# Head of the mixture-of-experts stage: row loads ahead of the last stores, gating inside the first tile's products, rows ahead of kept rows

## The chip, the cores and the metric

One core of a Trainium2 chip runs the whole program. The metric is device time in microseconds of one launch. Smaller is better. TensorE (PE) multiplies, with its weight loads beside it (PEld); VectorE (DVE) and ScalarE (ACT) do elementwise work and read the products out of PSUM; GpSimd (POOL) issues the indirect DMAs (scatters) and does some elementwise work; SyncE (SP) issues all other DMAs, in order.

## The reference

Three stages work one after the other on 8 batches of 3072 tokens of 256 numbers.

```python
X = np.fft.rfft(x, axis=1)                      # spectral mixing
Yr = Xr @ w_r - Xi @ w_i + b_r; Yi = Xr @ w_i + Xi @ w_r + b_i
Y = softthreshold(Yr, 0.01) + 1j * softthreshold(Yi, 0.01)
x = np.fft.irfft(Y, n=3072, axis=1).reshape(24576, 256)

c = x @ w_skip > 0                              # mixture of experts, 8 experts, one a token
e = argmax(x @ w_gate); g = softmax(x @ w_gate)[e]
x[c] += g * (relu(x @ w1[e]) @ w2[e])           # w1: 256x1024, w2: 1024x256

h = maximum(maximum(x @ w1, x @ w2), x @ w3)    # dense stage, 256 -> 768 -> 256
out = h @ w_out
```

## The kernel before

**Spectral stage** (`spectral`). A batch is transformed by small matrix products; the last step of a batch is a loop over `g` in 0..8. In round `g` the inverse transform `if1` (L353) makes a slice, and `to_rows` (L362) turns the slice of the round before into three blocks of 128 tokens, `yk[:, 3(g-1)]` to `yk[:, 3(g-1)+2]`, with gate scores beside the 256 numbers. Each block is stored at once to `xt` in DRAM by a 128 KB DMA (L372) on SP, so 24 stores a batch. `gating` (L379) is a generator: three steps on DVE (ten instructions, L385 to L412, which end with the mask `gm`), a step with a product for the column sums (L419) and two ACT instructions, then a step with the products L427 and L429 that give the places (nine DVE instructions, L431 to L446), after which the blocks stand in a list. `scatter(n, behind)` (L463) lets POOL wait for the tile `behind` and then scatters up to `n` blocks of the list into `rows`, a DRAM table sorted by expert.

In the last batch the gating is cut into five pieces (`LAST`, L567): blocks 0-2, 3-8, 9-14, 15-20 and 21-23. A piece is started in the round in which its last block is ready and finished in the next round.

**Experts stage** (`Experts`). It works on tiles of 256 rows of one expert. `tile` (L884) loads the tile's kept rows `xr` (`load_kept`, one DMA of 264 KB, for the residual, the gate weight and the target), then the transposed-to-be rows `xs` of the *next* tile (`load_rows`, four DMAs of 64 KB), both on SP. Four groups of 12 products each (L898, banks B, C, D, B) make `h`; after each, ACT writes `hh` (L903) and DVE `hl` (L904). After the fourth, `transposes` (L847) turns the next tile's `xs` to `xt` on DVE, splits it into `xh` (ACT) and `xl` (DVE), and `targets` makes `idx`. Then two times 24 products (L922) make `y`, and DVE makes `ob` from `y` and `xr` (L928). `tile` is a generator that yields after each group and in the middle and at the end of each half of `y`, so that its caller can put other work between. `send` (L862) scatters `ob` on POOL.

Each operand is split into a high and a low part (`h` and `l` at the end of the names); three products of them stand for one in full precision.

The first `HEAD` = 4 tiles of expert 0 (`head`, L939) are run from `spectral`'s own pools before a hardware loop over the other tiles. Their rows come from earlier batches, so their loads do not wait for the last batches' scatters. `open` (L779) loads, before the last rounds `g`, the rows of the first head tile and expert 0's weights. `get_ready(g)` (L854) splits `w1` in rounds 0 and 1, `w2` in rounds 2 and 3, and runs `transposes` for the first tile in round 4. `head` takes the last gating piece from its fourth step on, and then `table` (L969), which computes from the counts where each tile of the loop starts: DVE work on few partitions, loads of the first loop expert's weights in its second step, a product L1057 near its end. One step of that is taken at each yield of the tiles.

After the head, `loop` (L1064) runs the other tiles, and `tail` (L1092) the last two; the dense stage (`feed_forward`) follows.

What sets the order: all of this is in a manually ordered region, so each engine runs its instructions in the order of the program, and SP issues its DMAs in that order.

## Time and profile before

| | us |
|---|---|
| median of 3 runs | 2897.82 (2896.19 to 2897.95) |
| the profiled execution | 2884.95 |
| its span, first to last instruction | 2883.2 |

The profile gives times in us from the start of the span. Shares of the page: PE is busy 98% of the span, DVE 64%, ACT 48%, POOL 42%. The page's 40 slices show PE at nine tenths or more in all but three slices. The work that the change touches lies between about 744 and 857 us; the loop over the other tiles follows to about 1361, the two last tiles to 1390, and the dense stage to the end.

### The profile page before, as it was taken

How to read it: one execution, taken by the hardware profiler on the slowest of the kernel's cores; microseconds unless marked ns; L12 is line 12 of the kernel's file. 1: busy time of each engine (PE TensorE's matmuls, PEld its weight loads, DVE VectorE, ACT ScalarE, POOL GpSimd, SP SyncE). 2: the span in 40 equal slices, each digit the busy share in tenths (PEclk: the TensorE clock that was granted, in tenths of full speed). 3: DMA queues.
4: the chain of work that ended last, by engine and by line, in shares of the span. 5: the costliest groups of instructions: out<-in, count | busy, mean ns of one | idle time of the engine just before them, and what ended most of it. 6: DMA issues, size and time to landing. Idle time of an engine off the chain costs nothing.

```text
span 2883.2 us, 52001 instructions
## 1 busy us (share of the span) xinstructions
PE 2820.4 (98%) x17046; PEld 2446.7 (85%) x17047; DVE 1847.6 (64%) x2734; ACT 1381.2 (48%) x2665; POOL 1221.9 (42%) x1166
## 2 busy tenths in 40 slices
PE   9999999999979999999899999999999999999998
PEld 7888988998879999999777777777777777777776
DVE  6888788877755555555566666665666666666664
ACT  4544544454523333333455555555555555555553
POOL 2042224222542222222455555555555655555653
PEclk9999999999989999999999999999999999999999
DMA  5333333333254333333666667656677666676654
GB/s 159 102 103 114 115 116 101 107 100 101 87 179 126 103 104 97 106 96 103 136 168 159 174 171 177 169 159 170 166 179 175 164 168 160 177 173 176 160 153 106
DMA packets 401316, 400.75 MB, mean 139 GB/s; under 512 B 272634, under 2 KB 319303, under 8 KB 401140
## 3 DMA queue, kind: packets, MB, share of 16 engines
q1 hardware_dynamic: 386612, 371.63, 47.9%
q0 software_dynamic: 14528, 26.85, 2.7%
q8 instruction: 101, 1.65, 0.2%
q14 instruction: 75, 0.61, 0.1%
HBM read 309.52 MB, written 101.91 MB: 143 GB/s over the span
## 4 chain that ended last, share of the span: by engine, by line
PE 46%; DVE 3%; ACT 1%; issue 1%; DMA 1%; POOL 0%; POOLq 0%; DVEq 0%; ACTq 0%
PE pa L1216 19%; PE o_ps L1294 12%; PE pb L1216 10%; PE pc L1216 5%; DVE m L1262 1%; ACT hh L1273 1%; DVE xl L1175 1%; DMA wu<-wsc 1%; DVE m L1226 0%; ACT xh L1172 0%; DVE xc L1154 0%; DVE xt L1159 0%; POOL hl L1274 0%; DMA xt<-ob,idx 0%; POOL xt L870 0%
## 5 line engine op out<-in xcount | busy, mean ns | idle before, releaser
L1216 PE MATMUL pa<-xh,wu 128*128 128x512 f32 x1728 | 611.4, 394 | 3.4 <-ACT s L1223 2.5
L1223 ACT ACTIVATE s<-pa 128x512 f32<-128x512 f32 x648 | 378.9, 596 | 332.3 <-PE pa L1216 207.2
L1274 POOL TENSOR_TENSOR hl<-m,hh 128x512 fp32r<-128x512 f32 x288 | 400.7, 1413 | 297.1 <-ACT hh L1273 297.1
L1216 PEld LDWEIGHTS pa<-xh,wu 128*128 128x128 f32 x1728 | 324.5, 188 | 81.5 <-ACT s L1223 3.4
L1216 PE MATMUL pb<-xh,wu 128*128 128x512 f32 x864 | 345.2, 400 | 8.0 <-DVE m L1226 6.5
L1294 PE MATMUL o_ps<-hh,wo 128*128 128x512 f32 x1152 | 339.8, 397 | 3.4 <-ACT hh L1273 3.4
L1216 PE MATMUL pa<-xl,wu 128*128 128x512 f32 x864 | 339.7, 393 | 0.0
L1253 POOL TENSOR_TENSOR t<-s,s 128x512 f32<-128x512 f32 x144 | 188.3, 1308 | 258.7 <-ACT s L1223 258.7
L1294 PEld LDWEIGHTS o_ps<-hh,wo 128*128 128x128 f32 x1152 | 217.5, 189 | 54.7 <-ACT hh L1273 4.5
L1223 ACT ACTIVATE s<-pb 128x512 f32<-128x512 f32 x216 | 129.3, 598 | 265.4 <-PE pb L1216 264.9
L1262 DVE TENSOR_TENSOR m<-m,t 128x1536 f32<-128x1536 f32 x144 | 251.9, 1749 | 0.0
L903 ACT ACTIVATE hh<-h_ps 128x512 fp32r<-128x512 f32 x192 | 114.0, 598 | 267.8 <-PE h_ps L898 197.7
L904 DVE SCALAR_TENSOR_TENSOR hl<-h_ps,hh 128x512 fp32r<-128x512 f32 x192 | 131.3, 691 | 156.4 <-ACT hh L903 154.4
L472 POOL DMA_INDIRECT rows<-yk,pos x192 | 195.1, 1016 | 84.8 <-issue 59.4
L898 PE MATMUL h_ps<-xh,w1h 128*128 128x256 f32 x768 | 213.0, 277 | 7.6 <-ACT xh L145 5.1
L1216 PEld LDWEIGHTS pb<-xh,wu 128*128 128x128 f32 x864 | 162.2, 188 | 63.6 <-DVE m L1226 15.9
L922 PE MATMUL y_ps<-w2l,hh 128*128 128x256 f32 x768 | 212.9, 277 | 0.7
L898 PE MATMUL h_ps<-xl,w1h 128*128 128x256 f32 x768 | 213.0, 277 | 0.3 <-DVE xl L148 0.3
L898 PE MATMUL h_ps<-xh,w1l 128*128 128x256 f32 x768 | 212.8, 277 | 0.0
L922 PE MATMUL y_ps<-w2h,hh 128*128 128x256 f32 x768 | 212.1, 276 | 0.0
L922 PE MATMUL y_ps<-w2h,hl 128*128 128x256 f32 x768 | 212.1, 276 | 0.0
L1273 ACT ACTIVATE hh<-m 128x512 fp32r<-128x512 f32 x288 | 165.6, 626 | 82.4 <-DVE m L1262 82.4
(290 smaller groups left out, 7062.8 us busy)
## 6 DMA issues: line engine op xcount, KB each, us to landing
wu<-wsc SPq DMA_DIRECT2D x216, 896.0 KB
xc<-in_x_dram SPq DMA_DIRECT2D x64, 384.0 KB
xt<-yk SPq DMA_DIRECT2D x192, 128.0 KB
xs<-xt SPq DMA_DIRECT2D x192, 128.0 KB
out_dram<-ob SPq DMA_DIRECT2D x192, 128.0 KB
xr<-rows SPq DMA_DIRECT2D x52, 264.0 KB, 2.9
xs<-rows SPq DMA_DIRECT2D x208, 64.0 KB, 2.4
w1f<-in_moe_w_dram SPq DMA_DIRECT2D x10, 1024.0 KB
```

Of the source, the lines that this page charges most:

```text
L472: a = nc.gpsimd.indirect_dma_start(out=rows[:, :], out_offset=bass.IndirectOffsetOnAxis(ap=pos, axis=0), in_=yk[:, t, G:G + RW], in_offset ...
L898: nc.tensor.matmul(p[:, j], lhsT=a[:, k, f0:f0 + 128], rhs=v[:, k], start=(i == 0), stop=(i == 5))
L903: nc.scalar.activation(out=self.hh[:, sl], in_=p, func=AF.Relu)
L904: nc.vector.scalar_tensor_tensor(out=self.hl[:, sl], in0=p, scalar=0.0, in1=self.hh[:, sl].bitcast(F32), op0=ALU.max, op1=ALU.subtract,)
L922: nc.tensor.matmul(y, lhsT=a[:, c, 128 * j:128 * j + 128], rhs=v[:, c], start=(i == 0), stop=(i == 23))
L1216: nc.tensor.matmul(o, lhsT=self.w[:, g, at:at + 128], rhs=v[h], start=(start and i == 0), stop=(i == 2), skip_group_check=True,)
L1223: nc.scalar.activation(out=self.s[k], in_=o, func=AF.Copy)
L1253: nc.gpsimd.tensor_tensor(out=self.t[:, 2], in0=self.s[5], in1=self.s[7], op=ALU.add)
L1262: nc.vector.tensor_tensor(out=m[:, 0:3], in0=m[:, 0:3], in1=self.t, op=ALU.max)
L1273: nc.scalar.activation(out=hh[:, i], in_=m[:, i], func=AF.Copy)
L1274: nc.gpsimd.tensor_tensor(out=hl[:, i], in0=m[:, i], in1=hh[:, i].bitcast(F32), op=ALU.subtract)
L1294: nc.tensor.matmul(o, lhsT=wo[g][:, 2 * p + c, 128 * k:128 * k + 128], rhs=h[v][:, (0, 3, 1, 2)[2 * t + c]], start=(p == 0 and i == 0), st ...
```

## The change

- `load_kept` of the first head tile moves to `open`, behind its `load_rows` and ahead of the weights.
- `get_ready`: `transposes` of the first tile moves from round 4 to round 0, and behind it stands `load_rows` of the second head tile, ahead of the batch's 24 stores on SP. The splits of `w1` move to rounds 1 and 2, of `w2` to rounds 3 and 4.
- Round 8 no longer advances any gating. The fourth and later steps of the piece 15-20 and all of the piece 21-23 go into `head`, one step at a yield of the first tile; `table` follows.
- `tile` loads the next tile's rows ahead of the kept rows, in the loop and the tail too, and yields once behind the loads. The first head tile loads nothing.
- The scatters of a head tile, two and two, go behind the first and the fourth group of products (before: the first and the third).
- The loads of the first loop expert's weights move from `table`'s second step to the start of the third head tile, behind its row loads. `table` takes one more yield, so that L1057 goes to the middle of the second tile's first half of `y`.

```diff
-            queue = []
+            queue, gates = [], []
@@ rounds g of the last batch
-                        if late:
+                        if late and g < 8:
                             next(late[1], None)
                         if g in LAST:
-                            for _ in late[1] if late else ():
+                            for _ in late[1] if late and g < 8 else ():
                                 pass
                             late = [g, gating(b, *LAST[g])]
-                            for _ in range(3):
+                            gates.append(late[1])
+                            for _ in range(3 if g < 8 else 0):
                                 next(late[1])
-                        elif late:
+                        elif late and g < 8:
...
-            ex.head(bank, late[1], scatter)
+            ex.head(bank, gates[-2:], scatter)
@@ open
         self.load_rows(self.head_rows[0], True)
+        self.load_kept(self.head_rows[0], True)
         self.load_w1(0)
@@ get_ready
-        if g < 2:
-            self.split_w1(512 * g, 512 * g + 512)
-        elif g < 4:
-            self.split_w2(4 * g - 8, 4 * g - 4, True)
-        elif g == 4:
+        if g == 0:
             self.transposes()
+            self.load_rows(self.head_rows[1], True)
+        elif g < 3:
+            self.split_w1(512 * g - 512, 512 * g)
+        elif g < 5:
+            self.split_w2(4 * g - 12, 4 * g - 8, True)
@@ tile
-        self.load_kept(kept(), early[0])
         if ahead:
             self.load_rows(ahead(), early[1])
+        if kept:
+            self.load_kept(kept(), early[0])
+        yield None
...
-        if ahead:
+        if turn:
             self.transposes()
@@ head
         def rest():
-            yield from gate
-            yield
-            yield from ends
+            for n, g in enumerate(gates):
+                if n:
+                    for _ in range(3):
+                        next(g)
+                yield
+                next(g)
+                yield
+                for _ in g:
+                    pass
+                yield
+            yield from self.table(bank)
...
             for n, behind in enumerate(now):
-                if behind is not None and n % 2 == 0:
+                if n == 0:
+                    if j == HEAD - 2:
+                        for _ in rest:
+                            pass
+                        self.first_weights()
+                    continue
+                if behind is not None and n in (1, 4):
                     scatter(2, behind)
                 next(rest, None)
@@ table
-        e_first = self.value(first_i, E - 1, [ET.SP])
-        self.load_w1(e_first)
-        self.load_w2(e_first)
+        self.first_i = first_i
...
         yield
+        yield
         p = bank("A", (3, NTMAX))
         nc.tensor.matmul(p, lhsT=ones, rhs=q)
@@ new
+    def first_weights(self):
+        e_first = self.value(self.first_i, E - 1, [ET.SP])
+        self.load_w1(e_first)
+        self.load_w2(e_first)
```

## Rows read from the trace of the kernel before

**Rows 1.** Windows: us, then busy us (x instructions) of PE, PEld, DVE, ACT, POOL; clock, DMA.
```profile
806.70:857.10 50.40, 37.59 (x291) 36.00 (x291) 25.24 (x73) 11.81 (x20) 17.41 (x26) 0.83 0.61 191
857.10:1360.70 503.60, 502.90 (x4416) 501.29 (x4416) 263.17 (x459) 170.46 (x290) 133.74 (x200) 1.00 0.38 107
```

**Rows 2.** Timeline of PE: start, us, line, [idle before <- releaser].
```profile
785.76 0.24 PE L419 MATMUL bankA<-ones,gm 128*54 128x128 f32 x1 [1.46 <-DVE gm L412]
...
791.66 0.24 PE L419 MATMUL bankA<-ones,gm 128*54 128x128 f32 x1 [1.05 <-DVE gm L412]
...
792.48 0.39 PE L898 MATMUL bankB<-xh,w1h 128*128 128x256 f32 x1
...
796.12 0.22 PE L419 MATMUL bankA<-ones,gm 128*27 128x128 f32 x1 [2.00 <-DVE gm L412]
...
815.02 0.58 PE L898 MATMUL bankB<-xh,w1h 128*128 128x256 f32 x1 [8.35 <-ACT xh L145]
...
821.82 1.39 PE L1057 MATMUL bankA<-q,ones 8*128 8x318 f32 x2 [3.36 <-DVE q L1038]
```

**Rows 3.** Windows, PE alone: the third head tile.
```profile
834.18:845.06 10.88, 10.88 (x98) 1.00 0.66 212
```

**Rows 4.** Windows at the changes of the granted clock, columns as in the first group.
```profile
795.40:809.08 13.68, 10.54 (x87) 10.31 (x87) 4.45 (x18) 2.17 (x5) 4.66 (x9) 1.00 0.48 131
809.08:826.14 17.06, 7.62 (x28) 6.20 (x29) 8.09 (x42) 1.23 (x2) 4.55 (x7) 0.50 0.44 140
...
1379.10:1382.51 3.41, 3.08 (x14) 2.92 (x14) 1.29 (x4) 0.10 (x1) 1.39 (x3) 0.50 0.31 74
```

**Rows 5.** Timeline of SP, DMA issues: the last load of `open`, stores, head loads.
```profile
750.50 0.45 SPq L815 DMA_DIRECT2D w2f<-in_moe_w_dram  x1
769.15 35.56 SPq L372 DMA_DIRECT2D xt<-yk  x24
804.92 1.15 SPq L844 DMA_DIRECT2D xr<-rows  x1
806.34 3.09 SPq L839 DMA_DIRECT2D xs<-rows  x4
```

**Rows 6.** Timeline of DVE: gating of blocks 21-23, the second tile's transposes, the table, a late `hl`.
```profile
794.32 0.18 DVE L385 TENSOR_TENSOR glg<-yk 128x27 f32<-128x27 f32 x1
...
795.82 0.16 DVE L412 TENSOR_SCALAR gm<-gcmp 128x3 fp32r<-128x3 f32 x1
...
813.59 0.71 DVE L848 STREAM_TRANSPOSE xt<-xs 128x512 f32<-128x512 f32 x1 [11.21 <-DMA xs<-rows]
...
815.70 0.10 DVE L975 MEMSET sums<- 8x48 f32 x1
...
821.42 0.26 DVE L1038 TENSOR_SCALAR q<-grid,own 8x106 f32<-8x106 f32 x1
...
840.52 0.69 DVE L904 SCALAR_TENSOR_TENSOR hl<-bankB,hh 128x512 fp32r<-128x512 f32 x1 [0.67 <-ACT hh L903]
```

**Rows 7.** Timeline of SP and PE in the tail.
```profile
1371.58 0.36 SPq L844 DMA_DIRECT2D xr<-rows  x1
1372.57 2.96 SPq L839 DMA_DIRECT2D xs<-rows  x4
...
1378.87 0.40 PE L898 MATMUL h_ps<-xh,w1h 128*128 128x256 f32 x1 [5.06 <-ACT xh L145]
```

**Rows 8.** One loop tile: SP's issues, DVE's `idx` and next `hl`; last, the DMA view.
```profile
892.15 0.34 SPq L844 DMA_DIRECT2D xr<-rows  x1
893.18 3.13 SPq L839 DMA_DIRECT2D xs<-rows  x4
...
900.83 0.17 DVE L937 CAST idx<-xr 128x2 int32<-128x2 f32 x1 [0.52 <-DVEq L1086]
...
903.67 0.69 DVE L904 SCALAR_TENSOR_TENSOR hl<-h_ps,hh 128x512 fp32r<-128x512 f32 x1 [1.58 <-ACT hh L903]
...
xr<-rows SPq DMA_DIRECT2D x52, 264.0 KB, 2.9
```

More of the change, by code (lines that the diff above doesn't have):

```diff
@@ L882, in send, with tile @@
             tc.declare_no_dep(a.ins, group="sent", reason="no token is in two tiles")
-    def tile(self, hps, yps, kept, ahead=None, weights=None, next_w1=None, early=(False, False), idx_last=False):
+    def tile(self, hps, yps, kept, ahead=None, weights=None, next_w1=None, early=(False, False), idx_last=False, turn=True):
         nc = self.nc
-        self.load_kept(kept(), early[0])
         if ahead:
             self.load_rows(ahead(), early[1])
+        if kept:
+            self.load_kept(kept(), early[0])
+        yield None
         for c in range(4):
@@ L937, in targets, with head @@
         self.nc.vector.tensor_copy(out=self.idx, in_=self.xr[:, :, 257:258].rearrange("p s o -> p (s o)"))
-    def head(self, bank, gate, scatter):
+    def head(self, bank, gates, scatter):
         hps = lambda c: bank("BCDB"[c], (2, TM))
         yps = lambda j: bank("CD"[j], (D,))
-        ends = self.table(bank)
         def rest():
-            yield from gate
-            yield
-            yield from ends
+            for n, g in enumerate(gates):
[9 more added lines that the diff above has]
+            yield from self.table(bank)
         rest = rest()
@@ L957, in head @@
                 self.send()
+            ahead = None
+            if last:
+                ahead = lambda: self.value(self.t_row[0:1, 0:1], E * CAP - TM, [ET.SP])
+            elif j:
+                ahead = lambda: self.head_rows[j + 1]
             now = self.tile(
-                hps, yps, lambda: self.head_rows[j],
-                (lambda: self.value(self.t_row[0:1, 0:1], E * CAP - TM, [ET.SP])) if last
-                else (lambda: self.head_rows[j + 1]),
+                hps, yps, (lambda: self.head_rows[j]) if j else None, ahead,
                 None, self.split_w1 if last else None, (True, not last), last,
@@ L1100, in tail @@
             self.send()
-            for _ in self.tile(self.hps, self.yps, lambda: row(nt + 1)):
+            for _ in self.tile(self.hps, self.yps, lambda: row(nt + 1), turn=False):
                 next(prepare, None)
```

## The prediction

> **What bounds the kernel now.** I read the windows first. In the loop over the tiles PE is busy for 502.90 of 503.60 us, so nothing but fewer products would help there; in the 50.4 us before it, which hold the last three head tiles, PE is busy for 37.59 us, at a mean granted clock of 0.83 [rows 1]. The change works on this stretch and on the some 20 us ahead of it. Next I read PE's timeline there, for what ended each wait [rows 2]. Three times PE reaches a gating piece's column sums (L419) before DVE has made the mask `gm`: 1.46, 1.05 and 2.00 us. Then it waits 8.35 us for the second head tile's `xh`, and in that tile 3.36 us for the table's `q` ahead of L1057. An undisturbed head tile, the third, takes 10.88 us for its 96 products, 0.113 us for one [rows 3].
>
> The 8.35 us are SP's. The 24 stores of the last batch keep SP busy from 769.15 for 35.56 us, to 804.7. Behind them stand the first tile's kept rows, at 804.92, and only then the second tile's rows, at 806.34, which land at 813.59, 4.2 us after their last issue [rows 5, 6]. The table's first DVE work stands behind these transposes on DVE (815.70), and so `q` (821.42 to 821.68) comes late too: the 3.36 us have the same root [rows 2, 6]. The clock pays once more: it is granted at 0.50, the 1.2 GHz level, from 809.08 to 826.14 [rows 4].
>
> **What the change removes.** (1) *The second tile's rows* go to SP in round 0, when the first tile's transposes have freed `xs`. SP issues nothing between the last weights at 750.50 and the first store at 769.15 [rows 5], and four issues take about 3.1 us. They cost nothing as long as DVE reaches the transposes in that gap; if it doesn't, each late us delays the stores by as much. So tile 2 finds its `xh` ready: **-8.35**. (2) *The table* no longer stands behind a DMA: most of the 3.36 goes; what is left is worked out in (6). **-3.36**. (3) *The half clock* of 809.08 to 826.14. The second tile starts at 815.02 and the third at 834.18 [rows 2, 3], 19.16 us; less 10.88 and the wait of 3.36 that is 4.9, of which L1057 itself, 1.39 us at the lower clock, is worth 0.7 at the higher. **-4.2**. (4) *The first two mask waits.* In round 4 the transposes with their detour over ACT make way for a split of `w2`, and DVE can begin the piece 9-14 about 1.3 us earlier: the same transposes hold DVE for 2.1 us at 813.59 to 815.70, with ACT's `xh` in the middle [rows 6], and a split has no such detour. Of 1.46 I leave 0.2, bounds 0 and all of it. The wait of 1.05 ahead of tile 1 goes, since that product now stands behind tile 1's second group, 2.7 us later. The third wait, 2.00, moves to (5). **-1.3 -1.05 -2.00.** Together -20.2 us.
>
> **What it adds.** (5) *A longer mask wait in tile 1.* The piece 21-23 has its three DVE steps at the yield behind the fourth group, and its product L419 in the middle of `y`'s first half, 12 products or 1.36 us of PE time later. On DVE that mask stands behind the group's `hl` and behind the second tile's transposes and `idx`. From the last product of a fourth group to the end of its `hl`: tile 3 starts at 834.18, 48 products later is 839.6, and its `hl` ends at 841.21, so 1.6 us [rows 3, 6]. The nine instructions that finish the piece 15-20 stand ahead of that `hl` and overlap with its wait: +0.6, an estimate from the ten mask instructions, which take 1.66 us (794.32 to 795.98). From the transposes to the end of `idx` 2.1 us (813.59 to 815.70), of which ACT's `xh` is a part. The mask: 1.66 [rows 6]. That is 6.0 us, 6.15 with a semaphore, against 1.36: **PE waits 4.8 us**. The bounds are 3.9 (nothing of the finishing in the way, no gaps) and 5.5 (all of it in the way). Nothing hides it: PE has no other work in its order. Queued behind L419 are the rest of `y` and all later tiles.
>
> (6) *L1057* in the middle of the second tile's first `y` half: from the table's first instruction to the end of `q` DVE needs 6.0 us in the trace (815.70 to 821.68, two `ob` among them) [rows 6]; now it has from the end of tile 1's first `y` half to there, about 2.7 + 5.4 + 1.4 = 9.5 us, with four `hl`, two `ob` and the finishing of 21-23 between, about 5. A wait of **0.2**, bounds 0 and 1.5.
>
> (7) *The clock after 4.8 us without a product.* No row shows a wait of that size inside a tile. Behind the 5.06 us in the tail the clock is at 0.50 for 3.41 us; behind the 8.35 us for 17.06; behind the 2.00 us it stays at 1.00 [rows 2, 4, 7]. 4.8 is nearest to 5.06: 3.41 us at half the clock cost 3.41 x 0.5 = **1.7**. Bounds 0 and, with 17.06 us, 8.5. The Trainium skill (TensorE: Matmul & The Clock Gate, section "Why this matters for your kernels") warns of idle gaps between bursts in mid-kernel, because they bring the lower clock back; the trace agrees with the two dips above. It speaks against this change, which closes one long gap and leaves one of middle size; without the rule the time would be 1.7 lower.
>
> (8) *What is moved and costs nothing.* The early kept rows (264 KB) and row loads lie ahead of the first store. In tile 2 SP issues tile 3's rows at 804.9, where the kept rows stood; 3.1 us of issue and 4.2 to land make 812.2, and 2.1 us later, 814.3, tile 3 could start [rows 5, 6]. By the sum it starts later: tile 1 at about 789.3 (792.5 less the waits of (4) and the gating products that moved), tile 2 16.6 us later (10.88, 0.5 of gating products, 4.8, and 0.4 for smaller gaps) at 805.9, tile 3 another 11.8 later at 817.7, with the dip 819.4. So the stores hide behind the new wait, with 3 to 5 us to spare. The weights of the first loop expert now stand behind tile 4's rows; from there to their split behind tile 4's fourth group are some 14 us, and 2 MB at the 212 GB/s of [rows 3] take 10. If they came later, the loop's first tile would wait for the rest. POOL scatters the same number of blocks, the second pair one group later.
>
> (9) *The loop and the tail.* Rows ahead of kept rows change nothing for a PE that is busy throughout [rows 1]. In the tail, PE's 5.06 us end with `xh` of the last tile, whose rows SP issues at 1372.57 behind the kept rows at 1371.58 [rows 7]: they come 1.0 us earlier, **-1.0**. Bounds 0 and 1.0, since the kept rows' own issue is all that can be won.
>
> **The sum.** -20.2 + 4.8 + 0.2 + 1.7 - 1.0 = -14.5 us. The durations are those of the profiled execution (2884.95, span 2883.2), which was 12.9 under the median of the runs, 2897.82; I take the difference off the median: **2883.3**.
>
> **The rivals.** *B, no wait in tile 1*, because DVE gets through sooner than I read. Then the stores' queue is the bound: tile 3 starts at 814.3 instead of 819.4, 5.1 us better, 2878.2. For it: only the order on DVE makes the wait. Against: that order is written out, and each term of 6.0 is a row. *C, the half clock stays*: the dip lasts 17.06 us as before [rows 4], 8.5 instead of 1.7: 2890.1. For it: in the trace a second, shorter wait (3.36) kept it low, and L1057 could wait again. Against: 5.06 cost 3.41 us only. *D, the change doesn't do what it says*: the early rows wait after all (for scatters, or behind the stores), and the 8.35 and the half clock come back: -14.5 + 8.35 + 4.2 leaves about -2, 2895.9. Against: the second tile's rows at 806.34 go out 0.3 us after the kept rows' issue ends at 806.07 and land in 7.3, with no wait for the scatters that follow. *E, slower*: in each of the some 46 loop tiles (52 kept loads less 4 of the head and 2 of the tail [rows 8]) the kept rows now come behind four row issues. They would be issued at about 896 instead of 892.15 (rows at 892.15, 3.13 of issue, the register loads) and land 2.9 later, at 898.9. DVE's `idx` needs them at 900.83, and DVE is next needed at 903.67, with two `ob` of 0.5 us before that [rows 8]. So PE is touched only if they land after about 902.5, 6.5 us after issue instead of 2.9. From there each us costs 46; 0.35 us past it eats the gain, and 0.5 makes 23 - 14.5, 2906. For it: the weights share the queue. Against: they are issued behind the kept rows, and the median is 2.9.
>
> **How the numbers follow.** Chances: forecast 0.62, B 0.13, C 0.12, D 0.06, E 0.07. The forecast alone, with the bounds of (5) to (7) and (9), runs from 2880 to 2887. The range takes in B and C, 2877.5 to 2890.5, and leaves D and E out. A difference under about 0.2% (5.8 us) can't be told from no change: the forecast, B and C lie above that, less a little for a C that is longer; D is within. Faster 0.85, same 0.08, slower 0.07.
>
> **What the profile of the changed kernel would show.** Four row issues on SP ahead of the first store, and four behind the last, near 805. PE without the waits of 8.35 and 3.36; instead one of 4 to 5.5 us ahead of an L419 inside the first `y` half, released by DVE's `gm`, and behind it 0.50 for some 3.4 us. The loop starts 13 to 14 us earlier than at 857.1, and the wait in the tail is about 4. I am wrong if L419 waits for less than 2 us (B), if the clock stays low past one tile (C), if the second tile still waits for a DMA (D), or if PE has gaps in the loop at L898 or L922 (E).

## The result and the profile after

The kernel after takes 2873.12 us in the median of 6 runs (2871.94 to 2879.97), the kernel before beside it 2897.74 (2896.19 to 2898.83): a ratio of 0.9918, 95% interval 0.9908 to 0.9928, or 24.6 us. Forecast were 14.5 us and 2883.3, and the range ended at 2877.5. The profiled execution of after took 2872.75 us, its span 2871.0.

PE's timeline of after: start, us, line, [idle before <- releaser]. The first row is the only wait above 1.1 us that is left between the first head tile and the loop; the others are the first product of the third head tile, L1077 (L1057 of before), the first product of the loop and that of the last tile.

```profile
799.56 0.28 PE L419 MATMUL bankA<-ones,gm 128*27 128x128 f32 x1 [4.23 <-DVE gm L412]
...
806.53 0.28 PE L903 MATMUL bankB<-xh,w1h 128*128 128x256 f32 x1
...
813.42 0.80 PE L1077 MATMUL bankA<-q,ones 8*128 8x318 f32 x2
...
842.33 0.36 PE L903 MATMUL h_ps<-xh,w1h 128*128 128x256 f32 x1 [1.06 <-DVEq L1098]
...
1366.79 0.58 PE L903 MATMUL h_ps<-xh,w1h 128*128 128x256 f32 x1 [5.92 <-ACT xh L145]
```

SP's DMA issues of after: the second tile's rows stand ahead of the 24 stores, the third's right behind them, and a load of `wu`, the next stage's weights, stands at the loop's end, ahead of the last rows.

```profile
762.82 3.31 SPq L841 DMA_DIRECT2D xs<-rows  x4
767.41 39.17 SPq L372 DMA_DIRECT2D xt<-yk  x24
806.85 3.92 SPq L841 DMA_DIRECT2D xs<-rows  x4
811.02 0.40 SPq L846 DMA_DIRECT2D xr<-rows  x1
...
1349.13 0.40 SPq L1150 DMA_DIRECT2D wu<-wsc  x1
1355.54 4.15 SPq L1173 DMA_DIRECT2D xs<-xt  x8
1360.35 3.01 SPq L841 DMA_DIRECT2D xs<-rows  x4
```

Windows of after (us, then PE, PEld, DVE, ACT, POOL busy and instructions, granted clock, DMA share, GB/s): both stretches at half clock, the loop, and the tail with the way to the next stage.

```profile
797.92:804.75 6.83, 5.19 (x24) 5.14 (x25) 3.33 (x26) 0.38 (x2) 0.51 (x3) 0.50 0.34 96
1364.54:1371.36 6.82, 4.43 (x19) 4.14 (x20) 3.88 (x8) 1.23 (x2) 2.30 (x4) 0.50 0.71 238
842.33:1349.32 506.99, 504.52 (x4417) 502.95 (x4417) 263.06 (x461) 170.49 (x290) 134.26 (x201) 1.00 0.39 107
1349.32:1381.37 32.05, 25.11 (x193) 24.42 (x193) 16.49 (x25) 9.49 (x16) 9.63 (x12) 0.89 0.78 166
```

The waits of [rows 2] are gone, and 4.23 us (forecast 4.8) have come in their place. From the first of the last batch's four L339 products (752.92 before, 751.53 after) to the loop it was 104.18 us and is 90.80: **13.4 us less, where the prediction's sum for the head was 13.5**. Yet the two spans differ by 12.2 us only, 2883.2 to 2871.0, and the medians by 24.6. So half of the gain isn't in a comparison of these two traces. That the two sums for the head agree to 0.1 us is in part luck, since their misses cancel: the stretch ahead of the first tile is 3.48 us shorter, where (4) had 2.35, and the new wait is 0.57 shorter than forecast; against that the half clock costs some 1.7 us more, and the third and fourth tiles, for which the sum had nothing, take 11.31 and 12.53 us in place of 10.88 and 12.03.

### The profile page after: what moved, and what is told of

Same layout as the page of the kernel before. It is cut to its first block, busy times and chain, and to the rows that moved or that the text cites. A ratio compares the mean times of both kernels' runs of the same rounds, so it can differ in the third digit from the quotient of the medians.

```text
span 2871.0 us, 52049 instructions
## 1 busy us (share of the span) xinstructions
PE 2820.9 (98%) x17046; PEld 2449.0 (85%) x17047; DVE 1847.7 (64%) x2734; ACT 1381.0 (48%) x2665; POOL 1220.7 (43%) x1166
## 4 chain that ended last, share of the span: by engine, by line
PE 47%; DVE 3%; ACT 1%; issue 1%; DMA 1%; SPq 0%; POOL 0%; POOLq 0%; DVEq 0%; ACTq 0%
PE pa L1241 19%; PE o_ps L1319 13%; PE pb L1241 10%; PE pc L1241 5%; DVE m L1287 1%; ACT hh L1298 1%; DVE xl L1200 1%; DVE m L1251 0%; ACT xh L1197 0%; DMA wu<-wsc 0%; PE h_ps L903 0%; DMA xt<-ob,idx 0%; SPq L1173 0%; PE y_ps L927 0%; POOL hl L1299 0%
## 5 line engine op out<-in xcount | busy, mean ns | idle before, releaser
L472 POOL DMA_INDIRECT rows<-yk,pos x192 | 194.4, 1013 | 84.1 <-issue 59.3
```

What stands on the lines that cost most here:

```text
L472: a = nc.gpsimd.indirect_dma_start(out=rows[:, :], out_offset=bass.IndirectOffsetOnAxis(ap=pos, axis=0), in_=yk[:, t, G:G + RW], in_offset ...
```

## The experiments

The runs were made on five chips, A to E, in this order; all kernels of one group of runs shared a chip and the runs of before on it. Before's median was 2899.3 on A, 2909.5 on B, 2909.2 on C, 2900.4 on D and 2907.9 on E. Which chip the result's runs had isn't known; their 2897.7 for before go with A and D. The table has the median of each kernel, the time of its profiled execution, which can lie well off the median (11.1 us under it for the early rows on A), and the stages of that execution, in us (head: from the first L339 product of the last batch to the loop; tail: from the loop's end to the next stage's first product):

| kernel, chip | median | profiled | head | loop | tail |
|---|---|---|---|---|---|
| before, first profile | 2897.8 | 2884.95 | 104.2 | 505.2 | 29.9 |
| before again, A / D | 2898.1 / one run | 2898.5 / 2896.7 | 105.6 / 104.6 | 517.5 / 516.5 | 30.4 / 30.9 |
| after, first profile | 2873.1 | 2872.75 | 90.8 | 507.0 | 32.1 |
| early rows alone, A / D | 2887.5 / 2885.1 | 2876.3 / 2884.7 | 93.9 / 92.6 | 506.5 / 516.1 | 30.4 / 30.9 |
| gating earlier, A / D | 2876.9 / 2874.6 | 2877.3 / 2869.6 | 88.6 / 88.1 | 512.3 / 507.5 | 33.3 / 32.4 |
| kept rows first, A | 2880.1 | 2880.1 | 90.5 | 510.8 | 33.7 |
| loop order alone, C | 2902.5 | 2906.5 | 110.7 | 507.8 | 28.8 |
| after again, C / E | 2901.2 / 2897.3 | 2902.4 / 2897.6 | 98.9 / 99.3 | 515.7 / 511.1 | 32.4 / 33.1 |

**Where the other half is: the kernel before again.** No edit.

> The kernel before, unchanged. The profiled execution of before (2884.95) is 12.9 us under its median (2897.82), that of after (2872.75) stands at its median (2873.12): so the two traces explain 12.2 of the 24.6 us. Theory P (pace): products of 256 columns follow each other at two paces, 113.3 or 117.8 ns, which last over many tiles (after: 117.8 from about 815 to 884 us, before: 113.3 from 829 to 1361); in the timed runs of before the loop runs at the slow one for some 30 of 46 tiles, 0.43 us a tile. Then an execution near 2897 shows loop tiles of 11.31 us instead of 10.88, and head waits as in the trace shown. Theory G (gap): the wait for the second tile's rows and the half clock behind it are longer in the timed runs; then an execution near 2897 shows a wait of 12 us or more there, or 0.50 for 30 us or more, and loop tiles of 10.88. If this profile is near 2885 again it tells only that both states of before exist.

2898.06 us (2894.86 to 2900.26), ratio 0.9995 (0.9986 to 1.0005). Its head is 1.5 us longer than in the first profile, though the second tile waits 6.31 us for its rows in place of 8.35. The large difference is in the loop. PE alone in the same expert of the first profile and of this run, with an expert of this run that is like the first profile:

```profile
977.85:1043.13 65.28, 65.28 (x578) 1.00 0.34 93
```

```profile
980.02:1047.86 67.84, 67.84 (x579) 1.00 0.31 89
903.37:968.65 65.28, 65.28 (x578) 1.00 0.33 91
```

Six tiles of 96 products, PE never idle, the clock granted at 1.00 throughout, and yet 2.56 us apart: the products follow each other every 113.3 ns or every 117.8 ns (a tile in 10.88 or 11.31 us). In the first profile of before all eight experts have the faster pace; in this run six have the slower. That makes the loop 12.4 of the 13.6 us by which the two spans differ (2896.8 and 2883.2). The pace changes where PE has stood still, here before the first product that needs POOL's `w2l` at a change of expert (on average 113.3 ns from product to product before it, 117.8 behind; the rows give hundredths of a us only):

```profile
976.13 0.28 PE L922 MATMUL y_ps<-w2h,hh 128*128 128x256 f32 x1
976.25 0.28 PE L922 MATMUL y_ps<-w2h,hl 128*128 128x256 f32 x1
976.61 0.38 PE L922 MATMUL y_ps<-w2l,hh 128*128 128x256 f32 x1
...
977.07 0.28 PE L922 MATMUL y_ps<-w2l,hh 128*128 128x256 f32 x1
977.19 0.28 PE L922 MATMUL y_ps<-w2h,hh 128*128 128x256 f32 x1
977.31 0.28 PE L922 MATMUL y_ps<-w2h,hl 128*128 128x256 f32 x1
```

The same on D:

> The kernel before, unchanged, for its profile on the chip of these runs. Theory G (how long the second tile of the head waits for its rows depends on how fast the chip takes the last 24 stores, and after's gain with it): where the median of before is near 2909, the head's waits differ from those of the first profile, with 3 to 4 us for the rows in place of 8.35; where it is near 2898 they are 6 to 8.5. Theory P: the loop takes 505 us plus 0.43 for each tile at the slower pace beyond those of the first profile, within 0.5 us.

Before's median there was 2900.4, so that the first condition of theory G didn't hold, and its second did: the rows' wait is 7.10 us. The loop has 33 tiles at the slower pace against 9 (the tile that holds a change of expert counts among them): 505.2 + 24 x 0.43 = 515.5; measured 516.5, outside the 0.5 us by 0.5, since the tile at the entry (11.61 in place of 11.22) and those at the changes of expert are longer too.

**Is the pace drawn at each start?** Before, with the last pieces of each loop tile's first output half ahead:

```diff
-            for c in range(8):
+            for c in (6, 7, 0, 1, 2, 3, 4, 5) if weights and j == 0 else range(8):
```

> The kernel before, with the products of each loop tile's first output half taken in another order: the last two of the eight hidden pieces first. PE then stands still once in every tile, until ACT and DVE have made `hh` and `hl` of the last piece, about 1 us. It costs some 45 to 60 us; it is a way to make PE stop and start again 46 times in one execution. Theory P (the pace is drawn at each start, between two values and nothing else): behind the stops the products follow each other at 113.4 or at 117.8 ns, with nothing between, and the pace changes from tile to tile within one expert. Rival W (the pace belongs to the expert, to its weights or to a background activity of some tens of us): all tiles of an expert have one pace. Rival C (the pace is one of the granted clock): the slower tiles coincide with rows of a granted clock below 1.00.

2967.64 us, 67 more than before's median on D: PE stops twice a tile, for `hh` (0.84 us) and for `hl` (0.34). PE alone in four successive stretches between the stops, 93 steps from product to product in each:

```profile
915.37:925.92 10.55, 10.55 (x94) 1.00 0.23 65
927.99:938.54 10.55, 10.55 (x94) 1.00 0.23 64
940.67:951.22 10.55, 10.55 (x94) 1.00 0.21 63
953.32:964.27 10.95, 10.95 (x95) 1.00 0.25 66
```

Three stretches at 113.4 ns a step, the fourth at 117.7, and so on through nearly the whole loop: every fourth start gives the slower pace, whichever expert runs, two of them in a row only near 1310 us. W (it belongs to the expert) and C (the clock) fall. And the pace isn't random within an execution: with starts at nearly equal distances (12.6 us, 13.0 behind a slow stretch) it comes back regularly, as if it hung on the moment of the start against something periodic. What that is no row shows.

**Can the pace be steered?** Two changes of before in the loop, on B: POOL's `w2l` 0.2 us later, or two pieces more of it on DVE.

```diff
+            if c == 4 and not only:
+                nc.gpsimd.tensor_copy(out=self.seen[:, 0], in_=self.w2f[:, 4, 0:1])
```

> The kernel before, with one thing added in the loop: ahead of POOL's split of w2 at each change of expert a POOL copy of one element per partition, some 0.2 us, so that PE waits longer for `w2l` than it did. Nothing else moves. Theory P (PE's products follow each other at one of two paces, 113.4 or 117.8 ns, drawn anew where PE has stood still, and after a wait of 0.4 us or more it is nearly always the faster): the waits at the eight changes of expert grow by about 0.2 us each, 1.6 us in all, but an expert at the slower pace is followed by one at the faster, so that about half of the slow tiles go: 8 to 13 us faster than the kernel before, some 2885 to 2890. Rival W (a wait costs its own length and nothing else): 1.6 us slower, 2899 to 2900.

2910.33 us, ratio 1.0005 (0.9993 to 1.0017): no gain, a miss of theory P. The starts at the changes of expert did all lead to the faster pace, seven in its trace; but twice a hitch of 0.04 to 0.07 us one tile later (1145 and 1290 us) put PE back on the slower.

```diff
-            (nc.vector if c < 4 or only else nc.gpsimd).tensor_tensor(
+            (nc.vector if c < 6 or only else nc.gpsimd).tensor_tensor(
```

> The kernel before, with six of the eight pieces of w2's split on DVE in the loop and two on POOL, instead of four and four: `w2l` is ready earlier and PE doesn't wait for it at the change of expert. The same work. Theory P: the pace is then drawn once for the whole loop, or changes rarely; the loop stays at the pace with which it was entered, all experts alike. The executions fall into two groups, near 2880 to 2884 and near 2900 to 2903, or into one of them; the profile shows at most two of the eight experts with another pace than the rest. Rival W: the waits of about 0.37 us at eight places go, 1 to 3 us faster than the kernel before, all executions alike, unless DVE now comes late (up to 2 us slower).

2917.28 us, ratio 1.0027 (1.0015 to 1.0038): 7.8 us slower, though at five of the seven changes PE hardly waits any more, with 39 tiles at the slower pace. W said faster and falls. P's two groups of times didn't appear either (2912.52 to 2923.68): the pace still changes four times behind the entry. So the pace is worth up to 20 us (46 tiles x 0.43) to this loop, and neither edit set it.

**One part of the change alone: the early rows.** Before with the first tile's transposes in round 0, the second tile's rows and the first's kept rows ahead of the stores; gating, scatters, weights and the loop as before.

```diff
+        self.load_kept(self.head_rows[0], True)
...
+        if g == 0:
+            self.transposes()
+            self.load_rows(self.head_rows[1], True)
```

> Before, with the second tile's rows and the first kept rows early and the get_ready rounds shifted, nothing else: gating, weights of the first loop expert, order of loads in a tile and scatters as before. Theory of the prediction: the wait of 8.35 us goes, but the weights now stand ahead of the third tile's rows on SP, so about 5 to 7 us of wait come back at the third tile with half clock behind it: 5 to 9 us under before. Rival (early rows are all of it): 15 us or more under before.

2887.45 us, ratio 0.9962 (0.9947 to 0.9976); 11.8 of the 24.6 us. The head is 93.9 us, 10.3 to 11.7 less than before's. Its third head tile waits for no rows, against the expectation; the table's wait ahead of it is still 2.69 us. The profiled execution is not a typical one here: it took 2876.33 us, the other four 2886.94 to 2889.78, and its loop has the faster pace behind the first change of expert. On D it was run again:

> The kernel before with the early rows of the second tile alone, now on the chip of these runs. Theory G: where before's median is near 2909 its second tile waits 3 to 4 us for the rows instead of 8.35, and the early rows are worth 2 to 6 us (ratio 0.998 to 0.9993) instead of the 11 that were measured on the first chip; where it is near 2898 they are worth 9 to 12 again. Rival: 9 to 12 us on either chip.

2885.09 us, ratio 0.9949 (0.9934 to 0.9965), 15.3 us. Before waits 7.10 us for the rows on D, and the gain of the medians is above the 9 to 12 of theory G. Between the two profiled executions on D, whose loops are alike (516.5 and 516.1), it is 12.0, all of it in the head (104.6 to 92.6): this is the cleanest measure of the early rows. No chip with the shorter wait was met here, so that the first half of G stands untested by this run.

**The new wait: the last gating pieces one yield earlier.**

```diff
@@ rest in head, behind the three steps that make a piece's mask
-                yield
+                    yield
+                    yield
```

> After, with the steps of the two gating pieces one yield earlier and the mask of blocks 21-23 behind the third group of products, ahead of the transposes, so that L419 in the middle of the first y half finds it ready. Theory (the wait of 4.23 us in the first tile and the 6.83 us of half clock are paid): both go, 7.6 us, but the third tile's rows, issued behind the stores at about 807 to 811 and landed by about 814, end the next wait, of some 4 to 5 us, at the third tile: net 2 to 4 us under after. Rival (rows are not the bound): 7 to 8 us under after, about 2865. Rival (pace of PE decides): anything within 20 us, with loop tiles of 11.31 or 10.88 to show it.

2876.86 us, ratio 0.9926 (0.991 to 0.9943); on D

> The kernel after with the last gating pieces one yield earlier, as in the first experiment on the mask, now on the chip of these runs. Where before's median is near 2909 and after waits 7.66 us for the mask in the first tile: that wait and its dip of 6.83 us at half clock go (11 us), and 4 to 6 us come back at the loop's entry with its dip; 3 to 7 us under after's 2901 there, a ratio of 0.995 to 0.9965. Rival (the 7.66 us are not the mask's place on DVE but ACT or PE being late there): the wait stays at 3 us or more in the first tile, ratio 0.997 or above.

2874.57 us, ratio 0.9919 (0.9905 to 0.9933): no better than after on like chips (a chip like B, of which the second expectation speaks, was not met). The 4.23 us and their dip are gone, but the loop's first tile now waits; PE's, POOL's and SP's rows on A:

```profile
841.26 0.55 PE L903 MATMUL h_ps<-xh,w1h 128*128 128x256 f32 x1 [4.70 <-DVEq L1099]
```

```profile
812.10 1.01 POOL L873 DMA_INDIRECT xt<-ob,idx  x1 [11.81 <-DMA xs<-rows]
...
828.11 0.98 POOL L472 DMA_INDIRECT rows<-yk,pos  x1 [0.16 <-issue]
```

```profile
830.55 2.97 SPq L841 DMA_DIRECT2D xs<-rows  x4
```

POOL's first send of rows (L873) writes `xt`, which the 24 stores write too, and stands still until they have landed. That is a reading: the profile names a row load, but here as in after the send starts 7.1 to 7.2 us behind the end of the last store's issue (804.96 to 812.10; 806.58 to 813.78). The scatters (L472) behind it in POOL's queue end at 829.1, and the rows of the loop's first tile, issued at 830.55, stand behind them. After has a like wait of 10.47 us on POOL, but PE, which has its own 4.23 us, waits only 1.06 at the loop's entry. I had not named this queue.

**The scatters ahead of that send, and the tail.** The earlier gating, and all scatters in the first tile, on B; then the same with three `wu` loads ahead of the loop in place of two:

```diff
-                if behind is not None and n in (1, 4):
-                    scatter(2, behind)
+                if behind is not None and j == 0 and n in (1, 4, 8):
+                    scatter((2, 4, NBLK)[n // 4], behind)
```

> The kernel after, with the last gating pieces one yield earlier (as in the experiment on the mask) and all remaining scatters of the first tile's rows in the first tile, ahead of POOL's first send of rows, instead of spread over two tiles. What the experiment on the mask showed: its wait of 4.23 us in the first tile was gone, but 4.70 us came back at the loop's entry. Theory S (the first send waits for the stores' landing at about 812, POOL's scatters behind it come late, and the loop's first rows stand behind the last scatter): with the scatters ahead of the send the wait at the loop's entry falls from 4.70 to under 1.5 us, and its dip of 6.83 us at half clock goes or falls to 3.41. From the start of the stage to the loop 4 to 7 us less than in the experiment on the mask; at the same pace in the loop 2870 to 2873. Rival X (the loop's first rows wait for something else: the weights or the transfers' queue): the wait stays at 3.5 us or more and the time at 2875 to 2878.

```diff
-            for u in range(2):
+            for u in range(3):
...
-        load_weights()
+        with tc.manual_schedule():
+            load_weights()
...
-                if u + 2 < NU:
+                if u and u + 2 < NU:
```

> The same as the kernel with the early scatters, and the first three units of the next stage's weights (`wu`) are loaded ahead of the loop, as in the kernel before, instead of two ahead of it and one in the tail. Theory T (in the tail of the kernel after PE waits 5.92 us instead of 5.06 because a load of 896 KB stands ahead of the last rows): the wait in the tail falls to 4.0 to 4.6 us and the dip behind it from 6.83 to 3.41, 2 to 3.5 us less than the kernel without the early `wu` loads. Rival: the load is hidden, the tail stays at 5.5 to 6.5 us, and the earlier loads cost up to 2 us at the loop's entry.

2899.61 us, ratio 0.9959 (0.9942 to 0.9975), and 2897.94, ratio 0.9956 (0.9941 to 0.997). The loop's entry waits 0.99 us in place of 4.70, as theory S said. But PE also comes there later: a mask wait of 4.6 us is back in the first tile, 2.24 and 3.56 us stand ahead of the second tile's first `y` product, and the heads take 103.0 and 104.0 us. These waits alone could hide the one at the entry, so S isn't shown by these runs. On E the second kernel against after:

> The kernel after with the last gating pieces one yield earlier, all scatters of the last rows in the first tile, and no `wu` load between the loop and the last tiles: the edit of the kernel with the early scatters and `wu` loads, on the chip of these runs. Where before's median is near 2898 to 2900: against after no mask wait (4.23 us and its dip), no wait for the loop's first rows (the 4.5 us that came back without the early scatters), and a tail of 15.8 us in place of 17.5: 8 to 10 us shorter than after's execution in the head and tail, 2863 to 2867 at the faster pace throughout, 2865 to 2870 in the median. Where before is near 2909: 2896 to 2899 as measured. Rival: the first tile's mask waits 3 us or more as on the second chip, and the time is within 3 us of after.

> The kernel after, unchanged, on the same chip as the kernel with all four edits. Theory P: where before's median is near 2898 to 2900, its head from the anchor to the loop takes 13 to 14 us less than before's, and the median depends on how many experts run at the slower pace: 2871 to 2882, gain 17 to 27 us. Where before is near 2909: a gain of 6 to 10 us, as in the other run there. Rival H (the 24.6 us are the head's alone): 24 to 25 us on any chip.

2899.41 us, ratio 0.9967 (0.9957 to 0.9978), and after 2897.34, ratio 0.9965 (0.9952 to 0.9978): the same, as the rival said. PE's two long waits in the head of the kernel with all four edits:

```profile
817.46 0.28 PE L419 MATMUL bankA<-ones,gm 128*27 128x128 f32 x1 [3.62 <-DVE gm L412]
...
838.39 0.58 PE L927 MATMUL bankC<-w2h,hh 128*128 128x256 f32 x1 [4.11 <-issue]
```

The edits lose 4.8 us in the head (104.1 against 99.3 us) and win 2.5 in the tail (30.6 against 33.1); the loop of this execution is 3.8 us shorter (507.2 against 511.1), which is the pace again. A version that beats after wasn't found; this one never ran on A or D.

The tail is clearer. `wu` loads that stand between the loop and the last tiles delay what stands behind them on SP. PE's wait ahead of the last tile, with SP's rows, for the loop order alone (no such load) and for after with the three-unit edit, which went the other way there, two loads at that place:

```profile
1399.75 0.38 PE L901 MATMUL h_ps<-xh,w1h 128*128 128x256 f32 x1 [4.55 <-ACT xh L145]
```

```profile
1400.62 0.58 PE L903 MATMUL h_ps<-xh,w1h 128*128 128x256 f32 x1 [8.20 <-ACT xh L145]
...
1381.11 0.92 SPq L1150 DMA_DIRECT2D wu<-wsc  x2
1389.43 4.13 SPq L1173 DMA_DIRECT2D xs<-xt  x8
```

No load: 4.55 (and 4.70 in the kernel with early scatters and `wu`). One: 5.92 in after, 6.42 without the `wu` edit. Two: 8.20. The loads `xs<-xt` start 4.5, 6.2 and 8.1 us behind the tail's first product.

> The kernel after with one thing more: the first three units of the next stage's weights (`wu`) are issued ahead of the loop, as the kernel before has it, instead of one there and the rest in the tail. Theory T (the wu load of 896 KB ahead of the last rows ate the 1.0 us of the tail): the tail's wait falls from 5.92 to 4.0 to 4.9 us and the half clock behind it from 6.83 to 3.41; 2 to 3.5 us faster than the kernel after on the same chip. Rival: the wait stays at 5.5 us or more and the time within 1 us of after.

2904.94 us on C, ratio 0.9982 (0.9972 to 0.9991), 3.8 us above after there: the sign came out against theory T, because here the edit put one more load into the tail, which is 2.1 us longer than in after on C (34.5 against 32.4). Why the same edit brings all three loads ahead of the loop in the kernels with the early scatters and two of them behind it here, no row shows. A further kernel on C, with the same loads, the earlier gating, and POOL's first send behind the second tile's scatters, where the second tile's `idx` had already replaced the first's, so that the first tile's results go to other places:

> The kernel after with the early `wu` loads, the last gating pieces one yield earlier (their wait of 4.23 us and its dip go, as the experiment on the mask showed), and in the second tile all scatters still open ahead of POOL's first send of rows, which waits for the landing of the last stores. Theory S (the loop's first rows stood behind scatters which stood behind that send): no wait above 1.5 us in the head from the first tile to the loop's entry; the head 4 to 6 us shorter than after's, and 6 to 9 us under after in all, the lowest time of this study at the same pace. Rival X (the rows of the loop's first tile or of the fourth tile come late for another reason, or DVE is held because POOL sends the rows of tile 1 late): a wait of 3 us or more is back ahead of the third or fourth tile or at the loop's entry, and the time is within 3 us of the kernel with the early `wu` loads alone.

2908.06 us, ratio 0.9996 (0.9987 to 1.0005): a mask wait of 3.75 us, several of about 1 us, and 8.03 us in the tail. S isn't borne out in this form.

**The order in loop and tail.** After with the kept rows first again, on A, and before with that part of the change alone, on C:

```diff
+        if kept and not early[0]:
+            self.load_kept(kept(), early[0])
         if ahead:
             self.load_rows(ahead(), early[1])
-        if kept:
+        if kept and early[0]:
```

> After, with the kept rows ahead of the next rows again in the loop and the tail (the head as in after). The prediction: the loop is the same (10.88 us a tile either way), the tail's wait at xh is 1.0 us longer than in after: 0 to 1 us over after. Rival: the order in the loop matters for PE (loop tiles with waits); then several us under or over after with waits at L903 or L927 in the loop.

2880.06 us, ratio 0.9931 (0.9914 to 0.9947). The tail waits 7.03 us, 1.1 more than after's 5.92. But the kernel with the earlier gating, also on A and with the new order, waits 6.50. So the order is worth 0.5 to 1.1 us, near the 1.0 of step (9). The time is 6.9 us above after's in the result, not 0 to 1; 3.8 us of that are the loop's pace.

```diff
-        self.load_kept(kept(), early[0])
+        if early[0]:
+            self.load_kept(kept(), True)
         if ahead:
             self.load_rows(ahead(), early[1])
+        if not early[0]:
+            self.load_kept(kept(), False)
```

> The kernel before with one part of the change alone: in the loop and the tail the next rows are issued ahead of the kept rows. The head is as before. The forecast had nothing for the loop and 1.0 us for the tail. Theory N (the order matters in the tail only): 0.5 to 1.5 us faster than the kernel before, 2 to 4 of the eight experts at the other pace as in before. Theory Q (the order in the loop is what makes PE wait some 0.06 us longer for `w2l` at each change of expert in the kernel after, and so takes the next expert back to the faster pace): the waits ahead of the first product with `w2l` are 0.41 to 0.44 us from the faster pace and 0.17 to 0.20 from the slower, as in after, no expert at the slower pace is followed by another, and the time falls by 4 to 10 us.

2902.47 us, ratio 0.9971 (0.9962 to 0.998): 6.8 us. N's 0.5 to 1.5 is too little, but Q's sign of it is missing: the first product with `w2l` starts 0.38 us behind its forerunner, as in before, not 0.41 to 0.44, and a hitch of 0.13 us inside the second expert (at 961 us) brings the slower pace back. What brings the rest of the 6.8 us stays open; there is no trace of before on C.

**After on other chips.**

> The kernel after, unchanged, beside the kernel before on the same chip. Theory P (the median of before holds experts at the slower pace of PE, 117.8 ns a product, and after's executions hold fewer; the rest of the gain is the 12 to 13 us that the traces show): the ratio lies between 0.9915 and 0.9955, the gain between 13 and 25 us, and the profiled loop explains what exceeds 13 us: some 2.6 us for each expert at 117.8 ns less. Rival H (the whole 24.6 us is the head's, and the one profiled execution of before was not like the others there): the gain is 24 to 25 us again whatever the pace in the loop.

2901.17 us on C, ratio 0.9974 (0.9965 to 0.9983): 8.1 us, less than either theory gave; 10.6 on E. H falls, and so does the range of P. Two things differ on B, C and E. The head's gain is smaller: the kernels with before's head take 110.7 (C) and 109.7 us (B) for it, after 98.9 and 99.3. PE's rows of the loop order alone on C, of after on E, and ACT's of after on E:

```profile
830.74 0.58 PE L901 MATMUL bankB<-xh,w1h 128*128 128x256 f32 x1 [3.46 <-ACT xh L145]
```

```profile
811.61 0.28 PE L903 MATMUL bankB<-xh,w1l 128*128 128x256 f32 x1
...
820.98 0.28 PE L419 MATMUL bankA<-ones,gm 128*27 128x128 f32 x1 [7.73 <-DVE gm L412]
```

```profile
815.91 0.60 ACT L908 ACTIVATE hh<-bankB 128x512 fp32r<-128x512 f32 x1 [4.14 <-remote]
```

The stall that the early rows remove is 3.46 us there, not 8.35. From the anchor, the first L339 product, to the first head tile it is 45.5 us on C, 39.6 in the first profile of before; to the end of SP's stores 53.4 and 51.8. The tile starts 5.9 us later and the stores end 1.6 later, so that 4.3 of the 8.35 us are gone without any edit.

And the wait that the change adds is 7.73, not 4.23, because ACT's last `hh` of the tile starts 4.0 us behind the end of its group's last product (811.61 + 0.28; in the first profile of after 0.04 us). "remote" means that no instruction ends where the wait does. The wait is for PE's semaphore, and the trace has its update only at 815.89. Late updates are found for all engines on B, C and E: of the instructions of PE, ACT, DVE and POOL that end between 750 and 860 us and update a semaphore, 24 to 28% have no update in the trace within 0.2 us behind their end; on A, on D and in the first profiles it is at most 0.8%. The late `hh` of the second tile in the kernel with all four edits (7.42 us behind its group) is the same. Why the updates come late there, and whether they do without the profiler, isn't shown.

Secondly, after's loop there has experts at the slower pace like any other (515.7 and 511.1 us). The difference between the two kinds of chips itself lies mostly ahead of all this: the anchor comes at 751.5 to 753.4 us on A, on D and in the first profiles, at 762.7 to 765.9 on B, C and E.

## Why the prediction was wrong

The step that failed is the last one of the sum: **"The durations are those of the profiled execution (2884.95, span 2883.2), which was 12.9 under the median of the runs, 2897.82; I take the difference off the median"**. That assumes that the 12.9 us are the same in the kernel after, and with (9), which puts the loop at nothing, that the loop takes as long after as before. The 12.9 us are the pace of PE in the loop: in the profiled execution all eight experts ran at 113.3 ns, in the two profiled near the median six and five ran at 117.8 (the loop of before again on A is 12.4 us longer at the same work). After's median lies at a loop like that of its profile, 507.0 us with four tiles at 117.8 ns. Against an ordinary execution of before, that of A, after's span is 25.8 us shorter: 14.8 of it in the head, 10.6 in the loop, 1.4 in the dense stage, 0.6 ahead of the head, less 1.6 in the tail. So the loop, put at nothing, gave what the forecast lacked.

Against the first profile, which like after's holds no expert at 117.8 ns behind the first change, it is 12.2. I had explained the 12.9 by nothing and carried them over. Why before, by its times and two profiles, has the slower pace for some experts nearly always on A and D, and after hardly in the result, isn't settled. The early rows alone, on D, keep the slow loop (516.1), and after's own loop is slow in part on C and E. That the change itself makes the loop faster is therefore not shown: the head's share of the gain is explained, the loop's is only located.

Point by point, by the traces of the result:
- (1), (2), (4): right. The waits of 8.35, 3.36, 1.05 and 2.00 are gone, and 0.16 is left of the 1.46; the first tile takes 18.93 us in place of 22.53, the second 11.96 in place of 19.17. The early rows alone bring 10 to 12 us of the head's 13 to 15.
- (3), (7): the half clock of 17.06 us is gone, the dip behind the new wait is 6.83 us, twice the 3.41 that I took, inside the bounds; by an estimate at half speed it costs 1.7 us more. In the kernel with kept rows first the same wait, 4.24 us, is followed by 3.41. So the length of the wait alone doesn't set that of the dip. The Trainium skill (TensorE: Matmul & The Clock Gate, section "Why this matters for your kernels") says that idle gaps between bursts bring the lower clock back; both traces agree. Shorter waits can do it too: in before again on D the clock is at 0.50 for 3.41 us behind the mask wait of 1.99, where the first profile stayed at 1.00 behind 2.00.
- (5): 4.23, forecast 4.8, inside 3.9 to 5.5. (6): no wait at L1077, forecast 0.2.
- (8): held, but for an omission. POOL's queue counts: its first send waits for the stores, which I had passed over because POOL "scatters the same number of blocks". It cost nothing in after and ate most of the gain of the kernel with earlier gating.
- (9): the loop holds 507.0 us against 505.2, the four tiles at the slower pace behind its entry. The tail was forecast 1.0 shorter and is 2.1 longer: the order gave 0.5 to 1.1, and a weight load of 896 KB that moved from ahead of the loop to its end took back more. I had not looked at what the change does to loads that stand outside the manually ordered region.
- Rivals: B and C fell with the 4.23 us and the dip of 6.83; D with the five waits; E with a loop in which PE doesn't wait for kept rows.

## What to carry to other kernels

Before a difference is taken off a median, ask what sets the profiled execution apart from it: take a second profile of the same kernel and compare stage by stage, above all a stage in which PE is never idle. A step removed from one queue uncovers the next (here stores, then POOL's send, then the scatters), so follow a moved wait through every queue that it stood in, and look again at where the next stage's loads have gone. A gain of this size has a chip's share in it: 24.6 us here and 8 to 11 on others, from the same edit. Part of a gain can be a change of pace that nobody planned: count it apart.

## What the hardware showed

- At a granted clock of 1.00 the 256-column products follow each other every 113.3 or every 117.8 ns, constant from one stop of PE to the next; a hitch of 0.04 us was enough to change it. With stops at nearly equal distances every fourth start gave the slower pace.
- Two kinds of chips: before's median at 2898 to 2900 and at 2908 to 2910 us. On the second kind 24 to 28% of the semaphore updates of the head are not in the trace within 0.2 us of their instruction's end, on the first at most 0.8%; ACT started up to 7.4 us behind the end of the product that it read.
- A wait of 4.2 us was followed by 6.83 us at half clock in one execution and by 3.41 in another; one of 2.0 us by 3.41 and by none.
